# Opening loads in order from one queue, and a longer lag for the second matmul of a linear-attention block

## The chip, the cores and the metric

The kernel runs on one core of one Trainium2 chip. The metric is the device time of one execution in microseconds (us), the median of several runs. Times that I took from the trace's records, and not from its views, can differ from the views by 0.01 us.

Engines are called by their trace names in the profile lines: PE is TensorE (PEld its weight loads), DVE is VectorE, ACT is ScalarE, POOL is GpSimd, SP is the engine that issues most transfers (a q behind a name, as in SPq, means its queue of instructions).

## The reference

Inputs are bfloat16, x has 2048 tokens of 512 features. The output is a gated mix of two blocks. Only the first part of block `a` matters for the argument. The code is shortened.

```python
def reference(A_x, A_wqkv, A_wo, B_x, B_w1, B_b1, B_w2, B_b2, gate_w):
    g = sigmoid((x * gate_w).sum(-1, keepdims=True))
    # a: linear attention, 32 heads of 16
    q, k, v = heads(x @ wqkv)
    phi = lambda t: where(t > 0, t + 1, exp(t)) + 1e-6
    kv = einsum("bhsd,bhse->bhde", phi(k), v)         # sums over all 2048 tokens
    z = einsum("bhsd->bhd", phi(k))
    a = (phi(q) @ kv / (phi(q) . z + 1e-6)) @ wo
    # b: layernorm over features, then a two-layer MLP over the token axis
    b = mlp_over_tokens(layernorm(x))
    return g * a + (1 - g) * b
```

The kernel never forms v. It computes G = x^T phi(k), and multiplies G by the v weights afterwards. So its first stage needs, for each of 16 token tiles of 128 rows: K = x W_k (four matmuls, one for each slice of 128 features, called `kacc`), then phi on ScalarE and VectorE (result `pk`), then x^T phi(k) (four matmuls into four long-lived PSUM banks, `gacc`). The column sums z of all pk tiles are sixteen small matmuls (`zacc`) near the end of the stage. Then the MLP begins (`uacc`).

## The kernel before

The opening loads: four x tiles and the four slices of W_k, 128 KB each, alternately from the queues of SP and ScalarE. Token tiles 0 to 3 are transposed on TensorE, the others by DMA transposes.

```python
    for i in range(2):
        load_x(nc.sync, 2 * i, 1)
        load_x(nc.scalar, 2 * i + 1, 1)
    for i in range(2):
        load_wk(nc.sync, 2 * i)
        load_wk(nc.scalar, 2 * i + 1)
    load_xT(4, 2)            # DMA transposes, from SP
    load_xT(6, 2)
    # ... later loads, all from SP ...
    warm_up(6)               # six 128x512 matmuls on constants
```

The first stage. `k_phi` is an exp on ScalarE, then two VectorE instructions; `ln_step` is the layernorm statistics of one tile, also VectorE.

```python
    HEADS = 4
    transpose_tile(0, False)     # copied out of PSUM by VectorE
    transpose_tile(1, True)      # ... by ScalarE
    warm_up(1, 256)
    transpose_tile(2, False)
    transpose_tile(3, True)
    ln_step(0)
    ln_step(1)
    for k in range(ND - 1):              # slices 0, 1, 2 of tiles 0..3
        for t in range(HEADS):
            k_part(t, (k,))
    for t in range(HEADS):               # slice 3 of tiles 0..3
        k_part(t, (ND - 1,))
    for t in range(HEADS):
        k_phi(t)
    LAG = 4
    LN_LAG = 3
    for t in range(HEADS, NT):
        k_part(t, range(ND))
        k_phi(t)
        g_tile(t - LAG)                  # x^T phi(k) of an earlier tile
        if t > LAG:
            ln_step(t - LN_LAG)
        # ... load_small, ln_apply, ln_shift ...
    zacc = bank("zacc")
    for t in range(NT - LAG, NT):
        g_tile(t)
        if t == NT - 3:
            for u in range(NT):
                z_tile(u)
```

PSUM has eight banks here, all from one pool, used in turn. Completion of transfers is signalled on eight semaphores in turn, so that the ninth transfer has to wait until the first has landed (in the trace of before this holds SP for 0.7 us, until 3.41 us).

## Time and profile before

| | kernel before |
|---|---|
| median, 6 runs | 168.38 us (168.2 to 168.5) |
| span of the profiled run | 166.4 us |
| TensorE busy | 161.0 us, 97% |
| first K matmul | 6.25 us |
| ninth K matmul (first of slice 2) | 7.97 us |
| first MLP matmul (`uacc`) | 35.67 us |

From the page: busy time of each engine, and the shares of the chain that ended last.

```profile
PE 161.0 (97%) x798; PEld 74.3 (45%) x798; DVE 79.8 (48%) x189; ACT 58.3 (35%) x90; POOL 18.2 (11%) x37
...
PE 93%; DMA 3%; DVE 1%; SPq 1%; ACT 0%; issue 0%
```

TensorE is busy nearly all the time, so only its few waits can be won. They are in its timeline for the first 13 us (columns: start, duration, engine, line, operation, output and inputs, count; in brackets the idle time before, and what ended it):

```profile
0.85 2.72 PE L109 MATMUL wps<-const-bfloat16-1.0 128*128 128x512 bf16 x6 [0.85 <-PEq L487]
3.62 1.02 PE L198 MATMUL pt<-ident,xs 128*128 128x128 bf16 x8
4.45 0.30 PE L109 MATMUL wps<-const-bfloat16-1.0 128*128 128x256 bf16 x1
4.59 0.61 PE L198 MATMUL pt<-ident,xs 128*128 128x128 bf16 x8
6.25 4.48 PE L109 MATMUL kacc<-wk_sb,xT 128*128 128x512 bf16 x20 [1.05 <-DMA wk_sb<-in_A_wqkv_dram]
10.95 1.02 PE L109 MATMUL gacc<-pk,xs 128*128 128x512 bf16 x4 [0.23 <-DVE pk L212]
11.88 1.02 PE L109 MATMUL kacc<-wk_sb,xT 128*128 128x512 bf16 x4
```

TensorE waits 1.05 us for a slice of W_k, and 0.23 us for pk of tile 0. (A 512-column matmul lasts 0.38 us in the trace, but the next one starts 0.2155 us after it, so durations overlap; counted from the start of the matmul before, less these 0.2155 us, the second gap is 0.39 us.)

The chain of waits in the same stretch (start, duration, what), with the short steps left out:

```profile
1.75 4.45 DMA wk_sb<-in_A_wqkv_dram
...
6.25 2.98 PE kacc L109 x13
...
10.20 0.70 DVE pk L212
```

And the opening transfers (count, size, and median time from issue to landing):

```profile
xs<-in_A_x_dram ACTq DMA_DIRECT2D x2, 128.0 KB, 2.7
xs<-in_A_x_dram SPq DMA_DIRECT2D x2, 128.0 KB, 2.8
wk_sb<-in_A_wqkv_dram ACTq DMA_DIRECT2D x2, 128.0 KB, 4.4
wk_sb<-in_A_wqkv_dram SPq DMA_DIRECT2D x2, 128.0 KB, 4.6
```

### The profile page before, as it was taken

What the parts mean: (1) busy time and instruction counts of PE and PEld (TensorE: products, weight loads), DVE (VectorE), ACT (ScalarE), POOL (GpSimd) and SP (SyncE); (2) the same over time, 40 slices, a digit from 0 to 9 for tenths busy, and PEclk for the clock granted to TensorE, in tenths of its full rate; (3) what the DMA queues carried; (4) which work ended last, traced back from release to release, by engine and by line L of the source; (5) the groups of instructions that cost most, each with busy time, mean ns of one, the idle gap of its engine ahead of it and who ended that gap; (6) DMA issues with size and microseconds to landing.
All of it is one profiled execution on the core that took longest, in us unless ns stands there. A gap on an engine that the chain in (4) does not pass through costs nothing.

```text
span 166.4 us, 2087 instructions
## 1 busy us (share of the span) xinstructions
PE 161.0 (97%) x798; PEld 74.3 (45%) x798; DVE 79.8 (48%) x189; ACT 58.3 (35%) x90; POOL 18.2 (11%) x37
## 2 busy tenths in 40 slices
PE   7799999999999999999999999999999999999992
PEld 3434444434544444444444444444444444444461
DVE  1569999986986769992302412151222111111121
ACT  3263374927658557222222111051111222211110
POOL 5000512110020000002712521000000000000000
PEclk9999999999999999999999999999999999999999
DMA  5999999999900002900598499941100000110001
GB/s 157 229 256 255 348 354 310 349 349 345 242 1 2 0 0 65 357 23 32 185 294 196 138 322 262 309 159 63 35 32 32 32 33 32 46 52 32 32 32 32
DMA packets 29993, 25.05 MB, mean 151 GB/s; under 512 B 7776, under 2 KB 29408, under 8 KB 29984
## 3 DMA queue, kind: packets, MB, share of 16 engines
q1 hardware_dynamic: 27968, 22.02, 44.3%
q0 software_dynamic: 1440, 2.38, 5.6%
q10 hardware_dynamic: 576, 0.52, 1.1%
q8 instruction: 6, 0.10, 0.3%
q14 instruction: 3, 0.02, 0.0%
HBM read 21.11 MB, written 2.23 MB: 140 GB/s over the span
## 4 chain that ended last, share of the span: by engine, by line
PE 93%; DMA 3%; DVE 1%; SPq 1%; ACT 0%; issue 0%
PE uacc L109 29%; PE yps L109 29%; PE gacc L109 8%; PE qacc L109 8%; PE aps L109 8%; PE kacc L109 8%; DMA wk_sb<-in_A_wqkv_dram 3%; PE zacc L109 1%; PE denps L109 1%; PE kvps L109 1%; PE wps L109 1%; SPq L125 1%; DVE pk L212 0%; ACT e L208 0%; DVE ot L468 0%
## 5 line engine op out<-in xcount | busy, mean ns | idle before, releaser
L109 PE MATMUL uacc<-hs,w1c 128*128 128x512 bf16 x224 | 51.9, 379 | 0.0
L109 PE MATMUL yps<-uT,w2c 128*128 128x512 bf16 (+1 forms) x238 | 51.0, 367 | 0.0
L109 PEld LDWEIGHTS <-w2c 128*128 128x128 bf16 x238 | 23.3, 98 | 25.3
L109 PEld LDWEIGHTS <-w1c 128*128 128x128 bf16 x224 | 21.7, 98 | 26.2 <-issue 0.4
L468 DVE SCALAR_TENSOR_TENSOR ot<-yps,c,a_sc 128x512 bf16<-128x512 f32 (+1 forms) x17 | 12.1, 719 | 42.3 <-PE yps L109 41.4
L453 ACT ACTIVATE a_sc<-aps,c,gg 128x512 f32<-128x512 f32 x16 | 12.3, 777 | 46.8 <-PE aps L109 39.1
L415 DVE TENSOR_TENSOR pqT<-pqT,rex 128x512 bf16<-128x512 bf16 x16 | 6.5, 424 | 26.5 <-DMA rex<-rd_dram 26.5
L334 ACT ACTIVATE uT<-uacc,bcol 128x512 bf16<-128x512 f32 x14 | 9.3, 687 | 27.5 <-PE uacc L109 27.5
L109 PE MATMUL kacc<-wk_sb,xT 128*128 128x512 bf16 x64 | 15.8, 379 | 1.0 <-DMA wk_sb<-in_A_wqkv_dram 1.0
L109 PE MATMUL qacc<-xT,wq_sb 128*128 128x512 bf16 x64 | 16.4, 379 | 0.0
L109 PE MATMUL aps<-W2sb,pqT 128*128 128x512 bf16 x64 | 16.4, 379 | 0.0
L109 PE MATMUL gacc<-pk,xs 128*128 128x512 bf16 x64 | 15.9, 379 | 0.2 <-DVE pk L212 0.2
L248 ACT ACTIVATE hs<-xs,nmr,rstd 128x512 bf16<-128x512 bf16 x16 | 12.8, 805 | 3.1 <-DVE nmr L242 3.1
L209 DVE TENSOR_SCALAR e<-e 128x512 bf16<-128x512 bf16 x32 | 9.1, 284 | 9.1 <-ACT e L208 9.1
L208 ACT ACTIVATE e<-qacc 128x512 bf16<-128x512 f32 x16 | 9.6, 597 | 10.2 <-PE qacc L109 9.3
L208 ACT ACTIVATE e<-kacc 128x512 bf16<-128x512 f32 x16 | 9.0, 596 | 9.5 <-PE kacc L109 9.5
L212 DVE SCALAR_TENSOR_TENSOR pqT<-qacc,e 128x512 bf16<-128x512 f32 x16 | 11.1, 692 | 0.5
L212 DVE SCALAR_TENSOR_TENSOR pk<-kacc,e 128x512 bf16<-128x512 f32 x16 | 11.1, 692 | 0.6
L413 POOL DMA_DIRECT2D rex<-rd_dram x16 | 9.4, 593 | 15.9 <-DVE pqT L415 13.1
L232 DVE BATCH_NORM_STATS2 stats<-xs 128x6 f32<-128x512 bf16 x16 | 10.9, 683 | 0.0
L109 PEld LDWEIGHTS <-xT 128*128 128x128 bf16 x64 | 6.3, 98 | 8.6 <-ACT xT L202 1.2
L109 PEld LDWEIGHTS <-xs 128*128 128x128 bf16 x64 | 6.2, 98 | 8.4 <-issue 1.2
(66 smaller groups left out, 68.2 us busy)
## 6 DMA issues: line engine op xcount, KB each, us to landing
w2c<-in_B_w_dram SPq DMA_DIRECT2D x4, 1792.0 KB, 10.2
w1c<-in_B_w_dram SPq DMA_DIRECT2D x2, 2048.0 KB, 16.3
w1c<-in_B_w_dram SPq DMA_DIRECT2D x3, 1024.0 KB, 11.6
rex<-rd_dram POOLq DMA_DIRECT2D x16, 128.0 KB, 6.7
out_dram<-ot SPq DMA_DIRECT2D x15, 128.0 KB, 1.7
xs<-in_A_x_dram SPq DMA_DIRECT2D x3, 512.0 KB, 4.2
wq_sb<-in_A_wqkv_dram SPq DMA_DIRECT2D x1, 512.0 KB, 4.9
wv_sb<-in_A_wqkv_dram SPq DMA_DIRECT2D x1, 512.0 KB, 11.8
```

The costliest lines, as they stand in the source:

```text
L109: nc.tensor.matmul(o, lhsT=lhsT, rhs=rhs, start=start, stop=stop, **kw)
L125: q.dma_start(out=xs[:, t0 : t0 + n, :], in_=x_view[:, t0 : t0 + n, :])
L208: nc.scalar.activation(out=e[:], in_=acc[:], func=ACT.Exp)
L209: nc.vector.tensor_scalar(out=e[:], in0=e[:], scalar1=1.0, scalar2=PHI_EPS, op0=ALU.min, op1=ALU.add)
L212: nc.vector.scalar_tensor_tensor(out=dst, in0=acc[:], scalar=0.0, in1=e[:], op0=ALU.max, op1=ALU.add)
L232: nc.vector.bn_stats(out=stats[:], in_=xs[:, t, :])
L248: nc.scalar.activation(out=hs[:, t, :], in_=xs[:, t, :], func=ACT.Identity, scale=rstd[:, t : t + 1], bias=nmr[:, t : t + 1],)
L334: nc.scalar.activation(out=uT[:, j, :], in_=acc[:], func=ACT.Gelu_apprx_tanh, bias=bcol[:, j : j + 1])
L413: nc.gpsimd.dma_start(out=rex[:], in_=src.unsqueeze(1).to_broadcast([8, HEAD, SC]))
L415: nc.vector.tensor_tensor(out=seg, in0=seg, in1=rex[:], op=ALU.mult)
L453: nc.scalar.activation(out=a_sc[:], in_=aps[:], func=ACT.Identity, scale=gg[:, t : t + 1], bias=c2[:, t : t + 1],)
L468: nc.vector.scalar_tensor_tensor(out=ot[:, :W], in0=yps[:, :W], scalar=c1[:, t : t + 1], in1=a_sc[:, cs], op0=ALU.mult, op1=ALU.add,)
```

## The change

The intent: one queue delivers in order, so that what is needed first (x0, then x1, and so on, then slice 0 of W_k) comes first instead of sharing the transfer engines with what is needed later. And x^T phi(k) runs five tiles behind K instead of four, so that TensorE has a further K tile to do before it needs pk(0).

```diff
-    for i in range(2):
-        load_x(nc.sync, 2 * i, 1)
-        load_x(nc.scalar, 2 * i + 1, 1)
-    for i in range(2):
-        load_wk(nc.sync, 2 * i)
-        load_wk(nc.scalar, 2 * i + 1)
+    for t0, n in ((0, 1), (1, 1), (2, 2)):
+        load_x(nc.sync, t0, n)
+    for k0, n in ((0, 1), (1, 1), (2, 2)):
+        nc.sync.dma_start(
+            out=wk_sb[:, k0 : k0 + n, :], in_=wqkv_view[:, k0 : k0 + n, D : 2 * D]
+        )
...
-    LAG = 4
+    LAG = 5
...
-        g_tile(t - LAG)
-        if t > LAG:
+        if t >= LAG:
+            g_tile(t - LAG)
             ln_step(t - LN_LAG)
```

More of the change, by code (lines that the diff above doesn't have):

```diff
@@ L125, in load_x @@
         q.dma_start(out=xs[:, t0 : t0 + n, :], in_=x_view[:, t0 : t0 + n, :])
-    def load_wk(q, k):
-        q.dma_start(out=wk_sb[:, k, :], in_=wqkv_view[:, k, D : 2 * D])
     def load_xT(t0, n):
```

## The prediction

> **What bounds it now.** TensorE: 161.0 us busy of a 166.4 us span (busy table). The chain of waits is 93% TensorE; its one large foreign piece is a wk load, issued at 1.75 us, landing at 6.20. Timeline: warm-up matmuls 0.85 to 3.57, transposes of x tiles 0 to 3 from 3.62 to 5.20, 1.05 us idle, first K matmul at 6.25 (call that time K). A second idle piece, 0.23 us at 10.95, precedes the first x^T phi(k) matmul, waiting for pk(0). Then TensorE has no gap. So the change can touch about 1.3 us.
>
> **What changes, costed.**
>
> 1. Loads. Today SP and ACT each issue two x tiles and two wk slices, 0.44 us per issue. x lands 2.6 to 2.9 us after issue, wk 4.3 to 4.8; the first wk slices land at 6.0 to 6.2, the last at about 6.9. The Trainium skill ("DMA: Bandwidth & Descriptors", "Queues, rings and completion order") says that queues share 16 engines, which alternate between queues and take one queue's descriptors in order. Two queues thus mix slices 0 and 1; the trace agrees: pairs issued together land together. In order from SP, x0 should land at about 3.0, x1 3.5, x2-3 4.3, wk0 4.9 (4.5 to 5.5), wk1 5.4, wk2-3 6.3 to 6.7 (estimates from 350 GB/s between 2.5 and 3.5 us and the landings above). Issue costs SP about 2.8 us instead of 1.86, hardly binding.
>  The first four K matmuls need slice 0 alone, slice 1 is due at K+0.86, slices 2-3 at K+1.73. K is then limited by transposes and copies (TensorE done at 5.20 today; last copy 5.83, needed at K+0.65). K falls to 5.1 to 5.4: gain about 1.0 us.
>
> 2. Fewer transfers. SP no longer pauses 0.7 us before its first DMA transpose (until x0 lands: completion semaphores are reused after eight transfers). It starts at about 3.6 against 3.41 and lands 4.4 us later, 8.0; K tile 4 needs it at K+3.46, about 8.7. No stall.
>
> 3. Lag 5. TensorE runs K tile 5 before the first x^T phi(k), so the wait for pk(0) goes. But VectorE delivers pk only every 0.93 us here: pk(n) is done at K+4.64+0.93n. TensorE now reaches K tile 6 at K+6.05, and the built program has it wait for VectorE to free K tile 2's PSUM bank: pk(2), K+6.5. I expect about 0.45 us of wait there in place of 0.38 us before the first gacc matmul (10.57 to 10.95). To the end of the same work (K tiles 0 to 7, gacc tiles 0 to 2) it is K+9.94 before, K+10.0 after: worth nothing, within 0.1.
>
> **Carry-over.** Later loads have slack (first w1 half lands at 26.0, needed from about 35), VectorE moves with K, TensorE is gapless, so 1.0 us should reach the end.
>
> **Prediction: 167.4 us, range 166.8 to 168.1; faster by over 2%: 0.01, within 2%: 0.98, slower: 0.01.**
>
> **Right if:** the first kacc matmul starts at 5.1 to 5.4 with under 0.3 us idle before it; wk lands in order 0, 1, 2-3; the pk(0) wait is gone and 0.3 to 0.5 us of wait for pk stands before a kacc matmul near K+6.
>
> **Wrong if:** one queue alone moves data slower than two, so x2-3 or wk0 lands late; slices 2-3 land after K+1.73 and the wait only moves; the DMA transposes land late and K tile 4 stalls; VectorE's late pk tiles stall TensorE at the stage's end (tile 15 has 0.35 us of slack); or pk comes faster, and lag 5 gains its 0.3 us too.

## The result, and the profile after

A ratio is the mean time of one kernel's fast runs over that of the other's fast runs of the same rounds, so it is not quite the ratio of the medians.

| | before | changed |
|---|---|---|
| median, 6 runs each | 168.38 us (168.2 to 168.5) | 168.34 us (168.01 to 168.61) |
| ratio, 95% interval | | 0.9999 (0.9986 to 1.0011) |
| span of the profiled run | 166.4 us | 166.5 us |
| first K matmul | 6.25 us | 5.83 us |
| ninth K matmul | 7.97 us | 7.92 us |
| first `uacc` matmul | 35.67 us | 35.61 us |

The 1.0 us did not come. TensorE's timeline of the changed kernel:

```profile
0.85 2.72 PE L109 MATMUL wps<-const-bfloat16-1.0 128*128 128x512 bf16 x6 [0.85 <-PEq L484]
3.36 1.06 PE L195 MATMUL pt<-ident,xs 128*128 128x128 bf16 x8
4.21 0.42 PE L109 MATMUL wps<-const-bfloat16-1.0 128*128 128x256 bf16 x1
5.00 1.04 PE L195 MATMUL pt<-ident,xs 128*128 128x128 bf16 x8 [0.37 <-DMA xs<-in_A_x_dram]
5.83 5.70 PE L109 MATMUL kacc<-wk_sb,xT 128*128 128x512 bf16 x24
11.37 1.03 PE L109 MATMUL gacc<-pk,xs 128*128 128x512 bf16 x4
12.74 1.02 PE L109 MATMUL kacc<-wk_sb,xT 128*128 128x512 bf16 x4 [0.35 <-DVE pk L209]
```

Three things are to be seen. The first transposes start 0.26 us sooner. The second group starts 0.41 us later (5.00 instead of 4.59), after a wait for x tiles 2 and 3, and takes 1.04 us instead of 0.61: the array was still at half clock (0.107 us between starts). And the wait for pk has moved, from the first `gacc` matmul to a `kacc` matmul 1.4 us later (K tile 6, which needs the PSUM bank of K tile 2).

The chain of waits now runs through x, not W_k:

```profile
1.73 3.22 DMA xs<-in_A_x_dram
4.95 0.05 issue
5.00 1.04 PE pt L195 x8
6.04 3.13 PE kacc L109 x13
```

The transfers (the 256 KB ones are x tiles 2-3 and slices 2-3):

```profile
xs<-in_A_x_dram SPq DMA_DIRECT2D x2, 128.0 KB, 2.1
xs<-in_A_x_dram SPq DMA_DIRECT2D x1, 256.0 KB, 3.2
wk_sb<-in_A_wqkv_dram SPq DMA_DIRECT2D x2, 128.0 KB, 3.3
wk_sb<-in_A_wqkv_dram SPq DMA_DIRECT2D x1, 256.0 KB, 4.2
```

From the completion semaphores: x0 landed at 2.91 us (3.58 before), x1 at 3.42 (3.40), x tiles 2 and 3 together at 4.96 (4.19 and 4.00), slice 0 at 5.30 (6.21), slice 1 at 6.18 (6.02), slices 2 and 3 at 7.40 (7.00 and 6.72). That pairs issued together from two queues land nearly together, and those from one queue one after the other, agrees with the Trainium skill, "DMA: Bandwidth & Descriptors", "Queues, rings and completion order": each transfer engine takes turns between the queues that have work for it, and takes one queue's pieces in their order. (The page does not promise that they also complete in order; here all opening loads of a queue did, in every trace.) Ordering did what it should for x0 and slice 0. The bill came with tiles 2 and 3.

**The clock.** The trace file records when the array's clock gate opens fully. (The page's row of granted clock does not show this; it stands at full throughout.) It opened at 4.50 us in the trace of before, at 6.55 us in that of the changed kernel. Until then 512-column matmuls start 0.427 us apart, afterwards 0.2155 us. The Trainium skill, "TensorE: Matmul & The Clock Gate", Part 1, says that the gate opens after about 3.4 us of work, that the window that measures this runs free, and that the number of slow matmuls therefore differs between runs of one kernel. The traces agree: with the same first matmul at 0.85 us the gate opened at 4.50 us in one and at 6.55 in the other, and two traces of x_single below have 6.67 and 6.26. The gate then stays open for 163.84 us in the trace of before and for 160.43 us in each of the sixteen others: the two differ by 3.41 us, about one such window. Before, TensorE waited for W_k until 6.25, so the slow time was hidden. In the changed kernel K began at 5.83 and its first matmuls ran at half speed: the ninth came 2.09 us after the first instead of 1.72. So 0.37 of the 0.42 us of earlier start was lost at once. The half clock had already delayed that start: the first K matmul waits its turn behind the eight transposes, which took 0.83 us from 5.00. At 0.056 us apart, as before, they would have taken 0.44 us and K would have begun at about 5.44 (an estimate from these two traces; slice 0 had landed at 5.30).

**The stage's end.** VectorE's last pk tile and TensorE's z matmuls, kernel before (VectorE, then TensorE):

```profile
32.88 0.69 DVE L212 SCALAR_TENSOR_TENSOR pk<-kacc,e 128x512 bf16<-128x512 f32 x1
...
32.69 1.31 PE L109 MATMUL zacc<-pk,zsel 128*32 128x512 bf16 x16
```

and the changed kernel:

```profile
32.82 0.69 DVE L209 SCALAR_TENSOR_TENSOR pk<-kacc,e 128x512 bf16<-128x512 f32 x1
...
32.69 1.25 PE L109 MATMUL zacc<-pk,zsel 128*32 128x512 bf16 x16
```

In both, the last of the sixteen z matmuls starts 0.05 us after pk(15) is done (33.57 and 33.51 us). In both, pk(15) is done 22.67 us after pk(0), with no gap of VectorE over 0.04 us between them. And in both, 27.70 us pass from the ninth K matmul to the first `uacc`. So the new lag changed nothing, to 0.01 us, although the visible wait moved.

**The end of the kernel.** From the first `uacc` to the end it is 130.75 us before and 130.92 us after. TensorE's part is the same to 0.01 us. After the last store has landed, SP still checks the other completion semaphores one by one, 0.06 us each. The stores take these semaphores in turn, and with two opening transfers fewer the last one stands two places earlier in that row follow instead of four (1.28 us from the landing to the end instead of 1.16). The remaining 0.04 us is in that store's landing; I did not look for its cause.

The sum for the two profiled runs: 0.05 us gained up to the ninth K matmul, 0 in the stage, 0.17 lost at the end, together 0.11 us slower (166.42 and 166.53).

### The profile page after: what moved, and what is told of

The parts are those of the page before. It is cut to its first block, busy times and chain, and to the rows that moved or that the text cites. A ratio compares the mean times of both kernels' runs of the same rounds, so it can differ in the third digit from the quotient of the medians.

```text
span 166.5 us, 2085 instructions
## 1 busy us (share of the span) xinstructions
PE 161.6 (97%) x798; PEld 74.8 (45%) x798; DVE 79.7 (48%) x189; ACT 58.1 (35%) x90; POOL 18.3 (11%) x37
## 4 chain that ended last, share of the span: by engine, by line
PE 93%; DVE 2%; DMA 2%; SPq 0%; ACT 0%; issue 0%
PE uacc L109 29%; PE yps L109 29%; PE qacc L109 8%; PE aps L109 8%; PE gacc L109 8%; PE kacc L109 7%; DMA xs<-in_A_x_dram 2%; DVE pk L209 1%; PE zacc L109 1%; PE pt L195 1%; PE denps L109 1%; PE kvps L109 1%; PE wps L109 1%; SPq L125 0%; DVE e L206 0%; ACT e L205 0%
## 5 line engine op out<-in xcount | busy, mean ns | idle before, releaser
L398 DVE CUSTOM_DVE_ANT_0 junk<-xs,gw_b 128x512 bf16<-128x512 bf16 x16 | 9.9, 688 | 0.0
```

The source lines that it names most:

```text
L398: nc.vector.tensor_tensor_reduce(out=junk[:], in0=xs[:, t, :], in1=gw_b[:], scale=1.0, scalar=0.0, op0=ALU.mult, op1=ALU.add, accum_out=gp ...
```

## The experiments

The theory that I took into them, (A): the pk chain makes the lag worthless, and the merged transfer of x2-3 held back the loads. Its rivals: (B) lag 5 gained 0.3 us and the loads lost it again; (C) the half clock, not the landing, ate the gain of the loads. Up to four kernels ran on one chip, beside their own runs of before. The times come from five or six runs each, but landings and clock are known for the one profiled run alone.

### loads_lag4: the new loads, old lag

```diff
-    LAG = 5
+    LAG = 4
```

> The new loads with the old lag of 4. Theory A (lag 5 only moves a wait of 0.3 to 0.4 us from the first x^T phi(k) matmul to K tile 6): the time is that of the changed kernel within 0.15 us, 168.2 to 168.5; TensorE waits 0.2 to 0.5 us for pk before the first gacc matmul and not before K tile 6. Rival B (lag 5 gained 0.3 us and the loads lost it again): 168.6 to 168.8.

Measured: 168.10 us, ratio to before 0.9995 (0.9982 to 1.0008). From the ninth K matmul to the first `uacc` again 27.70 us, with the gap before the first `gacc` matmul as in before:

```profile
10.77 1.02 PE L109 MATMUL gacc<-pk,xs 128*128 128x512 bf16 x4 [0.23 <-DVE pk L209]
```

The clock opened at 6.63 us, the first K matmul started at 5.51, the ninth 2.28 us later. Theory A holds for the lag: B asked for 0.3 us or more above before, and the interval ends at 0.1. (The median lies 0.1 us under my range, but so does before in this call: 168.17, where it was 168.38.)

### lag_only: the old loads, new lag

```diff
-    LAG = 4
+    LAG = 5
```

> The old loads with lag 5. Theory A: 168.3 to 168.5, the wait for pk before the first gacc matmul is gone and one of 0.3 to 0.5 us stands before K tile 6. Rival B: 168.0 to 168.1.

Measured: 168.23 us, ratio 1.0006 (0.9994 to 1.0018). The wait stands before K tile 6, and the stretch is 27.69 us.

```profile
12.58 1.02 PE L109 MATMUL kacc<-wk_sb,xT 128*128 128x512 bf16 x4 [0.35 <-DVE pk L212]
```

### x_single: x tiles 2 and 3 as two transfers

```diff
-    for t0, n in ((0, 1), (1, 1), (2, 2)):
+    for t0, n in ((0, 1), (1, 1), (2, 1), (3, 1)):
         load_x(nc.sync, t0, n)
```

> The changed kernel with x tiles 2 and 3 as two transfers of 128 KB, still from SP alone in order. Theory A (the merged x2-3 transfer, landing at 4.96, held the transposes): x2 lands at 4.0 to 4.3, x3 by 4.7, transposes of tiles 2 and 3 run from about 4.5 to 5.5, the fourth K matmul, which started at 6.83, starts at 6.0 to 6.5, time 167.9 to 168.2. Rival C (the TensorE clock, not the load, sets the pace: the array runs at half speed until a window of its own phase closes, 6.55 in the changed kernel's trace and 4.50 in before's): the matmuls come earlier but those before the switch take twice as long, and the time stays within 0.15 us of the changed kernel's 168.3 where the switch is late.

Measured: 167.97 us, ratio 0.9986 (0.9971 to 1.0000). x2 landed at 3.92, x3 at 4.53, slice 0 at 4.92. TensorE's timeline:

```profile
4.21 0.42 PE L109 MATMUL wps<-const-bfloat16-1.0 128*128 128x256 bf16 x1
4.43 1.06 PE L195 MATMUL pt<-ident,xs 128*128 128x128 bf16 x8
5.28 6.03 PE L109 MATMUL kacc<-wk_sb,xT 128*128 128x512 bf16 x24
```

The wait before the transposes is gone and the first K matmul starts at 5.28, 0.97 us sooner than before: exactly what I had predicted for the change. But the clock opened only at 6.67 us in this trace, so the first three matmuls ran at half speed, the fourth started at 6.56 (I expected 6.0 to 6.5), and the ninth at 7.70. Of 0.97 us, 0.27 remained. Both the merged transfer and the clock are real, and the clock took the larger part here.

### x_single_2 and x_single_3: the same kernel again, for other positions of the clock

> The kernel with single x tiles a second time, for another position of the clock switch (6.67 us in the first trace). The first K matmul again at 5.2 to 5.4; the ninth comes 1.72 us plus half of the time to the switch later, plus at most 0.2 us for copies: 7.70 if the switch is late, 7.0 to 7.3 if it is before 5.5. The span moves by the same amount, within 0.15 us.

> The same kernel a third time, the same expectation: first K matmul at 5.2 to 5.4, ninth 1.72 us plus half of the time to the switch later (plus at most 0.2), and the span moves with it.

One look each (state unknown, so only the traces are used). In the second, the first K matmul came at 5.28 again, the clock opened at 6.26, the ninth matmul came at 7.49: 0.21 us sooner than in the first trace, and the span was 166.02 instead of 166.23, also 0.21 us less. The program and the start of the first K matmul were equal; what differed was the clock. In the third, slice 0 landed late (5.69 us), K began at 5.73, outside my range, when the clock (5.83) was nearly open: ninth at 7.48. A start 0.45 us later cost nothing.

### k_pairs: another order of the opening K matmuls

```diff
-    for k in range(ND - 1):
+    for k in range(ND - 2):
         for t in range(HEADS):
             k_part(t, (k,))
     for t in range(HEADS):
-        k_part(t, (ND - 1,))
+        k_part(t, (ND - 2, ND - 1))
```

K tile 0 is then complete after ten matmuls instead of thirteen, and VectorE's chain begins 3 x 0.2155 = 0.65 us sooner.

> The changed kernel, but the opening K tiles do slices 0 and 1 tile by tile and then slices 2 and 3 of one tile at once, so that K tile 0 ends three matmuls (0.65 us) sooner. Theory A (the pk chain of VectorE, which starts when K tile 0 ends and then runs at 0.93 us a tile, sets when TensorE is free of waits): pk(0) ends 0.5 to 0.65 us sooner after the first K matmul, the 0.35 us wait before K tile 6 goes, time 167.9 to 168.1. If something else holds the stage, the time stays at 168.3.

Measured: 167.40 us, ratio 0.9957 (0.9943 to 0.9970), more than I expected. TensorE's timeline shows no wait before K tile 6 (of four `gacc` records one is missing from the trace):

```profile
10.95 1.03 PE L109 MATMUL gacc<-pk,xs 128*128 128x512 bf16 x3
11.81 1.03 PE L109 MATMUL kacc<-wk_sb,xT 128*128 128x512 bf16 x4
```

The stretch from the ninth K matmul to `uacc` is 27.05 us instead of 27.70: the whole 0.65 us, not just the 0.35 to 0.39 us of the wait that I had looked at. pk(0) to pk(15) still takes 22.67 us. The stage as a whole moves with the start of VectorE's chain.

### pairs_oldloads: that order with the old loads and lag 4

The diff to the kernel before is that of k_pairs.

> The kernel before (old loads from two queues, lag 4) with the new order of the opening K matmuls alone. If the pk chain was what held the stage whatever the loads, the 0.2 us wait before the first gacc matmul goes and pk(0) ends 0.65 us sooner after the first K matmul: 0.4 us faster than before on this chip (0.3 to 0.5). If the gain needs the new loads: under 0.15 us faster.

Measured: 167.51 us, ratio 0.9951 (0.9930 to 0.9972), a gain of about 0.8 us where I expected 0.3 to 0.5. The stretch is again 27.05 us. So this gain needs neither the new loads nor the new lag. (The 0.65 us lies inside the interval.)

### pairs_x_single and pairs_x_single_lag4: everything together

The changed kernel with the edits of x_single and k_pairs; the second also with lag 4.

> x tiles singly, all from SP, lag 5, and the new K order. The gains should add: the first K matmul at about 5.3, no wait for pk. Time 0.8 to 1.2 us under before; in the profile the time from the first to the ninth K matmul is 1.72 us plus half of what lies between the first K matmul and the switch of the TensorE clock (plus at most 0.2 us for the copy of tile 3). Rival: a landing of wk slices 2-3 or the K tile 4 transpose stalls TensorE and no more than 0.6 us is gained.

> The same with lag 4. Once pk(0) is early enough, the lag should not matter: within 0.15 us of the lag 5 version and no wait for pk over 0.15 us. If lag 5 was needed to make room: 0.3 us or more slower, with the wait before the first gacc matmul back.

Measured: 167.07 us, ratio 0.9933 (0.9914 to 0.9952), and 167.08 us, ratio 0.9932 (0.9916 to 0.9948). On the same chip pairs_oldloads was at 167.51, so the single, ordered loads seem to be worth 0.3 to 0.4 us here (0.32 us between the means, and the two intervals overlap; the spans of the profiled runs differ by 0.34 and 0.41). The lag is worth nothing here either: 27.06 and 27.04 us. These two, with pairs_all_single below (167.11 on another chip), are the fastest kernels, about 1.1 us under before.

### changed_again: the changed kernel once more

> The changed kernel itself, for the same chip and for a second trace. Theory: within 0.2 us of before. If the trace shows a clock switch other than 6.55 us, the eight matmuls from the first K matmul take 1.72 us plus half of the time from it to the switch (plus at most 0.25 us while the copy of tile 3 is awaited), and the span is shorter with an early switch, by up to 0.4 us.

Measured: 167.96 us, ratio 0.9980 (0.9965 to 0.9995), just outside the 0.2 us that I expected. The clock opened at 5.96 us, x2-3 landed at 4.63 instead of 4.96, the first K matmul started at 5.50, the ninth at 7.49 (1.99 us later; the rule gives 1.95), and the span was 166.1 us. The whole 0.43 us between the two traces of this one kernel stands at the ninth K matmul already. So the change is worth between 0 and about 0.3 us, depending on the run.

### nowarm_before and nowarm_changed: no warm-up matmuls

```diff
-    warm_up(6)
```

> The kernel before without its six warm-up matmuls. [...]the first K matmul still starts at 6.0 to 6.3 (it waits for wk), the eight matmuls from it take 1.72 us plus half of the time to the switch, and the time rises by 0.3 to 1.6 us. If the clock does not matter here: no change, since TensorE waits for wk anyway.

> The changed kernel without its six warm-up matmuls. The first K matmul is as early as with them, 5.3 to 5.8, but more of the K matmuls run at half speed than in the version with the old loads, so that the earlier start is worth only half: the time rises by more than in nowarm_before or as much, and the difference between the two is under 0.5 us. If the clock does not matter: no change from the changed kernel.

Measured: 169.40 us, ratio 1.0079 (1.0052 to 1.0106), and 168.79 us, ratio to before 1.0043 (1.0026 to 1.0059). In the traces the clock opened at 6.99 and 6.91 us, and the ninth K matmul came 2.44 and 2.34 us after the first, as half the time to the switch demands. The first K matmul of nowarm_before came at 5.50 us, outside my range, as slice 0 landed at 5.46 in that run; its span is therefore that of before, 166.42 us. It was also the fastest of its runs, 168.47 us, and none of the slower ones was traced. So the warm-up matmuls earn their place by the times; that a later switch of the clock is what the slower runs paid for fits the rule but is not shown. My expectation about the difference missed: the changed kernel lost less than the old one, not more, and led by 0.6 us. A likely reason is that its TensorE begins work sooner (first transpose at 2.96 us instead of 3.54), which can bring the switch into an earlier window; the single traces do not show that, so it stays argued.

### pairs_all_single: all eight loads singly

```diff
-    for k0, n in ((0, 1), (1, 1), (2, 2)):
+    for k0, n in ((0, 1), (1, 1), (2, 1), (3, 1)):
```

(on top of pairs_x_single)

> The new K order, lag 5, and all eight opening loads singly from SP in order. wk slice 2 alone should land before the slices 2-3 together (6.9 us), at 6.2 to 6.7; TensorE needs it at 7.0 to 7.3, so the time stays within 0.2 us of the version with slices 2-3 merged (167.1): the loads are then no longer what limits.

Measured: 167.11 us, ratio 0.9942 (0.9923 to 0.9961), as expected. Slice 2 landed at 6.36 us. The time from the first `uacc` to the end is back at 130.75 us with eight opening transfers; it was 130.82 to 130.84 in all traces with seven and 130.91 to 130.92 in those with six, in the versions with the warm-up and the old place of the statistics. So each transfer fewer costs 0.08 us there: 0.06 us for one more semaphore check, and the rest in the landing of the last store.

### ln4_before and ln4_changed: one statistics step off VectorE's chain

```diff
-    LN_LAG = 3
+    LN_LAG = 4
...
+        if t > LN_LAG + 1:
             ln_step(t - LN_LAG)
```

(In the kernel before, the added line takes the place of `if t > LAG:`. `load_small`, which is called at a tile that depends on LN_LAG, moves one tile later too.)

> The kernel before with one layernorm statistics step (0.69 + 0.18 us of VectorE) put off from before pk(15) to the next stage. Theory (VectorE runs without a gap from pk(0) to pk(15), 22.66 to 22.67 us in every trace so far, and TensorE's last z matmul waits for pk(15), so this chain sets the end of the stage): pk(15) is 0.3 to 0.9 us sooner after pk(0), and the last z matmul comes over 0.2 us after pk(15) instead of 0.05; the time from the ninth K matmul to the first uacc matmul falls from 27.70 us to about 27.5, as only the waits at the start of the stage remain. Rival (TensorE's own work sets the end of the stage): it stays at 27.70.

> The same in the changed kernel. Theory: from the ninth K matmul to the first uacc matmul 27.5 to 27.6 us instead of 27.70; the 0.5 us wait before K tile 6 stays, as it lies before the first statistics step of the loop. Rival: 27.70.

One look each (state unknown; traces only). ln4_before, VectorE's last pk and TensorE's z matmuls:

```profile
31.87 0.69 DVE L212 SCALAR_TENSOR_TENSOR pk<-kacc,e 128x512 bf16<-128x512 f32 x1
...
32.73 1.05 PE L109 MATMUL zacc<-pk,zsel 128*32 128x512 bf16 x16
```

pk(15) is done 21.63 us after pk(0) instead of 22.67 (1.04 us, more than the 0.3 to 0.9 that I expected: the 0.17 us instruction `veps` moved behind pk(15) with the step), the last z matmul starts 0.83 us after it instead of 0.05, and the sixteen z matmuls take 1.05 us instead of 1.31: they had been waiting inside this group. The stretch falls to 27.43 us (old lag) and 27.50 us (new lag). So VectorE's chain was what ended the stage. Only with that taken away do the early waits show, and then lag 5 is 0.06 to 0.07 us the worse one, as its early wait is the longer (0.52 against 0.39 + 0.07 us, from the starts of neighbouring matmuls). With its waits taken off, each of the two stretches is 26.98 us. The gain does not last in this form: the put-off step costs 0.3 us in the next stage (131.05 us from the first `uacc` to the end instead of 130.75).

### All traces in one table

"Rule" is 1.72 us (eight matmuls at 0.2155) plus half of the time from the first K matmul to the opening of the clock, if that comes later.

| trace | clock opens | first K | ninth K | difference | rule | ninth K to `uacc` | pk(0) to pk(15) | span |
|---|---|---|---|---|---|---|---|---|
| before | 4.50 | 6.25 | 7.97 | 1.72 | 1.72 | 27.70 | 22.67 | 166.42 |
| changed | 6.55 | 5.83 | 7.92 | 2.09 | 2.08 | 27.70 | 22.67 | 166.53 |
| changed_again | 5.96 | 5.50 | 7.49 | 1.99 | 1.95 | 27.70 | 22.67 | 166.10 |
| loads_lag4 | 6.63 | 5.51 | 7.80 | 2.28 | 2.28 | 27.70 | 22.67 | 166.41 |
| lag_only | 5.46 | 6.03 | 7.76 | 1.72 | 1.72 | 27.69 | 22.67 | 166.21 |
| x_single | 6.67 | 5.28 | 7.70 | 2.41 | 2.41 | 27.70 | 22.67 | 166.23 |
| x_single_2 | 6.26 | 5.28 | 7.49 | 2.22 | 2.21 | 27.70 | 22.67 | 166.02 |
| x_single_3 | 5.83 | 5.73 | 7.48 | 1.75 | 1.77 | 27.70 | 22.68 | 166.02 |
| nowarm_before | 6.99 | 5.50 | 7.94 | 2.44 | 2.46 | 27.70 | 22.67 | 166.42 |
| nowarm_changed | 6.91 | 5.68 | 8.02 | 2.34 | 2.34 | 27.70 | 22.67 | 166.58 |
| k_pairs | 5.37 | 5.55 | 7.49 | 1.94 | 1.72 | 27.05 | 22.67 | 165.46 |
| pairs_oldloads | 6.03 | 6.04 | 7.76 | 1.72 | 1.72 | 27.05 | 22.67 | 165.57 |
| pairs_x_single | 5.71 | 5.28 | 7.26 | 1.98 | 1.94 | 27.06 | 22.68 | 165.16 |
| pairs_x_single_lag4 | 5.75 | 5.28 | 7.36 | 2.08 | 1.96 | 27.04 | 22.66 | 165.23 |
| pairs_all_single | 5.74 | 5.37 | 7.26 | 1.89 | 1.90 | 27.04 | 22.66 | 165.06 |
| ln4_before | 6.60 | 6.02 | 8.01 | 1.99 | 2.01 | 27.43 | 21.63 | 166.50 |
| ln4_changed | 4.93 | 5.25 | 7.19 | 1.94 | 1.72 | 27.50 | 21.62 | 165.84 |

Where the difference exceeds the rule by 0.2 us (k_pairs, ln4_changed), the clock was open early and TensorE had to wait for ScalarE's copy of transposed tile 3: the next limit. In pairs_x_single_lag4 slices 2-3 landed at 7.32 us, just before the ninth matmul, which cost 0.1 us.

## Why the prediction was wrong

It said 167.4 us (166.8 to 168.1); the result was 168.34.

- **Step 1, the loads: the step that failed.** The prediction put x tiles 2-3 at 4.3 us; the merged transfer landed at 4.96 (4.63 to 4.96 in the six traces of versions that keep it). It put the first K matmul at 5.1 to 5.4; it came at 5.83. With x2 and x3 sent singly it came at 5.28 in two of three traces, so the mechanism of ordered loads was right and the term mis-sized was the merged transfer: TensorE could not begin tile 2 until tile 3 had landed as well. Merging is not all of it: in the six traces with single tiles x3 still landed at 4.39 to 4.64, in the five with two queues the later of x2 and x3 at 4.19 to 4.46. With single tiles SP issues x3 at 2.20 us, where in before both x2 and x3 had been issued by 1.27; the prediction called the longer row of issues hardly binding. Whether they are what delays x3 was not tested. Slice 0 (4.9 predicted, 5.30) was within its range; slice 1 (5.4 predicted, 6.18) and slices 2-3 (6.3 to 6.7 predicted, 7.40) were late, but not needed sooner in this run.
- **The same step left out the clock.** It took all K matmuls at 0.2155 us, although the timeline of before showed slow and fast transposes side by side. Work that starts before the switch gains only half of its head start. In the profiled run this cost 0.37 us in the K matmuls, and about 0.39 us in the transposes before them (the estimate above); in x_single the K matmuls lost 0.69. (The two losses of the profiled run do not simply add up: with fast transposes the fourth K matmul would have waited for the copy of tile 3, as it did in ln4_changed, by 0.2 us. So how the missing 1.0 us divides between landing and clock is not settled.) The first two traces of x_single, which begin K at the same time, show it. So does ln4_changed, which keeps the merged transfer: there x tiles 2-3 landed at 4.65, the clock opened at 4.93, in the middle of the transposes, and K began at 5.25, inside the predicted range:

```profile
4.70 0.71 PE L195 MATMUL pt<-ident,xs 128*128 128x128 bf16 x8
5.25 5.56 PE L109 MATMUL kacc<-wk_sb,xT 128*128 128x512 bf16 x24
```

- **Step 2, fewer transfers: right.** The first DMA transpose was issued at 3.66 us without a pause and landed at 8.44 us (predicted 8.0); K tile 4 did not wait. Not foreseen: two fewer opening transfers lengthen the kernel's end by 0.12 us.
- **Step 3, the lag: right in size, wrong in part of its reason.** The wait moved to K tile 6, with 0.35 us idle (0.3 to 0.5 predicted), and the lag was worth 0.00 us. The prediction's own sum made lag 5 the worse one by 0.06 us, and that is what the two ln4 traces show. But the prediction also said that tile 15 had 0.35 us of slack at the end of the stage. It had none: the last z matmul waited for pk(15) in every version with the old place of the statistics, which is why the stage's length did not depend on the lag at all.
- **Carry-over: right.** What was gained at the ninth K matmul reached the end, less the 0.17 us of the kernel's end.

What stays open: why the landing of the same transfers differs by up to 0.8 us between traces of equal kernels (slice 0 of x_single: 4.92, 4.97 and 5.69 us), and whether the position of the clock switch can be influenced.

## What to carry to other kernels

When a start is moved forward, ask whether the clock of TensorE is already open there; before the switch a head start counts half. When TensorE shows several short waits in a stage, measure the other engine's chain from its first to its last result: if that is gapless and ends just before the consumer, an earlier start of that chain, or less work on it, shortens the stage, and shifting the waits about does not. (A later place for the consumer was not tried: the sixteen z matmuls stand before the `gacc` matmuls of tiles 14 and 15.) Merging transfers makes the consumer of the first half wait for the second.

## What the Trainium skill lacked or had wrong

- "TensorE: Matmul & The Clock Gate", Part 1, says that what is issued in the first 3.4 us or so runs at half clock, and that the transition "varies ±500ns". The half clock itself agrees (0.427 and 0.2155 us between starts). But with work from 0.85 us on, and no break over 0.6 us before the switch, the switch came at 4.50 to 6.67 us in 15 traces, 3.65 to 5.8 us after the first matmul: a range of 2.2 us, with 3.4 us below its lower end. That the cost is small enough to leave out of a model ("<1% of a typical kernel span", the same part) holds for the span, but not for a change that is worth 0.5%.
- "DMA: Bandwidth & Descriptors", "Rules for kernel authors", advises to coalesce many small transfers into one large transfer (it calls those under 64 KB mostly overhead; these had 128 KB). It has nothing of the cost seen here, a consumer that waits for the whole: two tiles merged to 256 KB landed at 4.63 to 4.96 us, where singly the first landed at 3.87 to 4.24 and the second at 4.39 to 4.64.
- No page has it that the order of completion semaphores shows at the end of a kernel: SP checks them one by one, 0.06 us each after the last store landed, 1.16 us in all with four checks left, 1.22 us with five and 1.28 us with six.
